# A later copy of the values' product, unread products before the MLP, and a last batch like the others: top-k attention and a channel MLP on one core

## The chip, the core and the metric

The kernel runs on one core of a Trainium2 chip. The metric is the time of one execution on the device, in microseconds (us). The kernel before takes 1666.45 us, the median of three executions (1665.65 to 1667.94). The execution that was profiled has a span of 1666.6 us. The engines are called PE (TensorE's matmuls; PEld are its weight loads), DVE (VectorE), ACT (ScalarE), POOL (GpSimd) and SP (SyncE, which starts most of the transfers).

## What is computed

Attention over 8 batches, 8 heads, 576 rows and a head dimension of 64, in which each row keeps only its 32 largest scores. The heads are then laid side by side (512 columns), and each row goes through a layer norm and an MLP of 512 to 2048 to 512 with a residual. All of it is in fp32.

```python
# attention: q, k, v are (8, 8, 576, 64)
scores = scale * np.matmul(q, k.transpose(0, 1, 3, 2))
kth = np.partition(scores, -32, axis=-1)[..., -32:-31]
scores = np.where(scores >= kth, scores, -1000000000.0)
scores = scores - np.max(scores, axis=-1, keepdims=True)
attn = np.exp(scores)
attn = attn / (np.sum(attn, axis=-1, keepdims=True) + 1e-09)
attn_out = np.matmul(attn, v)

# bridge, then the MLP: g_ln (512), w_ch1 (512, 2048), w_ch2 (2048, 512)
x = attn_out.transpose(0, 2, 1, 3).reshape(8, 576, 512)
mu = np.mean(x, axis=-1, keepdims=True)
var = np.mean((x - mu) ** 2, axis=-1, keepdims=True)
xn = (x - mu) / np.sqrt(var + 1e-06) * g_ln
out = x + np.maximum(xn @ w_ch1, 0.0) @ w_ch2
```

## The kernel before

The rows of a batch are cut into tiles of 128: numbers 0 to 3, and a rest of 64 rows, number J = 4. A **unit** is one tile for one pair of heads. There are 160 units, and the program is one loop over steps, one unit a step on DVE, with the other engines' work for the units before and after it written between. Nothing reorders the program: each engine takes its instructions in the order in which they stand in it.

A unit goes through these stages: `scores` (PE, with copies out of PSUM by ACT), `halve` and `select` (the 32 largest by rounds of MAX8 and MATCH_REPLACE8 on DVE, with two subtractions on POOL), `mask` and `weigh` (ACT: Prelu, then Exp with the row sum), and `turn` or `move` (the weights transposed, by PE and ACT or by DVE and DMA). Units of one batch and pair of heads form a **group**, and a group has one values' product:

```python
def values(g):
    vb = g.job.v
    av = brief("av")                       # a PSUM bank; five of these rotate
    for c in range(J):
        for h in range(2):
            nc.tensor.matmul(av[h * D : (h + 1) * D, 0 : g.nq], vb[:, h * J + c, :],
                             g.blocks[:, h, 0 : g.nq // 32, c, :], start=(c == 0), stop=False)
    nc.tensor.matmul(av[:, 0 : g.nq], g.job.ends[:], g.pt[:, 2 * J, 0 : g.nq],
                     start=False, stop=True)
    g.oT = otpool.tile([P, GQ], FP32, tag="oT", name="oT")
    nc.scalar.copy(g.oT[:, 0 : g.nq], av[:, 0 : g.nq])

def place(g):
    b, hp = g.job.b, g.job.hp
    for i, qt in enumerate(g.qts):
        if qt == J:
            ...                            # a copy of 64 columns on POOL
            continue
        ...
        ps = brief("xo")
        nc.tensor.transpose(ps[:, 0:P], g.oT[:, i * P : (i + 1) * P], ident[:])
        put(xs[b, qt], ps, hp * P, g.den, 2 * qt)     # two multiplications on ACT
```

When all pairs of heads of a tile are placed, the tile joins a **block** of one to three tiles for the MLP. A block's work is a list of items with a cost each, `todo`; `give` appends it at a fixed step, and `fill`, which is called eight times a step, takes items off the list as long as the allowance `owed` lasts. A `turn` item is four transposes on PE and a copy to xT on ACT. A `hidden` item is one 128-row product into hps; the last of each PSUM bank is followed by a relu on ACT. A `project` item is one product into ops; the last of each tile is followed by a scaling on ACT into o.

```python
def fill(least=0):
    owed[0] = min(owed[0] + share[0], 6.0)
    while todo and (not todo[0][3] or todo[0][3]()):
        if owed[0] < todo[0][1] / 2 and least <= 0:
            break
        least -= 1
        pop()                              # owed[0] -= cost; the item's instructions

# costs: turn 0.44, hidden max(1.71e-3 * N, 0.31) with N columns, project 1.71e-3 * 512

def slot(n):                               # share of one fill in step n
    if n <= CONVERTING:                    # CONVERTING = 17
        return max(0.0, dve_cost(n) - pe_cost(n)) / SLOTS       # SLOTS = 8
    left = sum(t[1] for t in todo)
    if n > last_give:
        even = left / max(1, END - 1 - n)
    else:
        even = 99.0
        for m in sorted(gives):
            if m > n:
                even = min(even, (left - RESERVE) / (m - n))    # RESERVE = 4.0
                left += sum(b.cost() for b in gives[m])
    return max(0.0, even) / SLOTS
```

The first block is given in step 9 (`gives_first`). Until then `todo` is empty. The order of the units comes from this list; `[0, 1]` and so on are the tiles of one group:

```python
for b in range(B):
    parts = [[0, 1], [2, 3], [J]]
    if b:
        parts = [[0, 1], [2, 3]]
        if b == B - 1:
            parts = [[J]] + parts
        else:
            parts[b < 2].append(J)
    for qts in parts:
        jobs += [Job(b, hp, [qts]) for hp in range(NHP)]     # NHP = 4 pairs of heads
...
for u in units[jobs[5 * NHP].first :]:                       # from batch 2 on
    u.moved = not u.rest and u is not u.group.units[-1]
```

A unit that is `moved` has its weights transposed by DVE and DMA. The others are transposed on PE, eight transposes for the two heads besides one for the last columns. The rests of an even and the following odd batch are put together to one tile, which joins the block of the odd batch's group that holds J; where that group holds nothing else, it is a block of one tile.

One step, cut to the order in which the calls concerned stand (ex is the unit of two steps ago, mk that of one step ago, g the group whose last unit came three steps ago):

```python
    for x in due(n): scores(x)
    ...
    fill()
    ...
    fill()
    if g: values(g)
    if parts and not moved: parts[0]()     # turn of ex, first head
    ...                                    # select, halve, the weights' conversion
    fill()
    if mk and not early: mask(mk, 0)
    if g: place(g)
    ...
    fill(1 if g or late else 0)
    fill()
    if len(parts) > 2: parts[1]()
    ...
```

Of the kernel before, what the change touches and what calls it, by code (L numbers as in the profile page):

```python
# [11 lines left out]
FP32 = mybir.dt.float32  # L12
# [9 lines left out]
J = 4  # L22
# [7 lines left out]
def kernel(  # L30
# [41 lines left out]
    nc = tc.nc  # L72
    P = nc.NUM_PARTITIONS
    B, H, S, D = q.shape
# [15 lines left out]
    GQ = 2 * P + R  # L90
# [11 lines left out]
    otpool = pool("ot", 1)  # L102
# [22 lines left out]
    def product(name):  # L125
        return mmps.tile([P, 512], FP32, tag="mm", name=name)
# [5 lines left out]
    ident = const([P, P], "ident")  # L132
# [72 lines left out]
    now = [-1]  # L205
# [38 lines left out]
    share = [0.0]  # L244
    owed = [0.0]

    def done(step):
        return step is not None and step < now[0]

    def pop():  # L250
        kind, cost, run, may = todo.pop(0)
        assert not may or may()
        owed[0] -= cost
        run()
# [5 lines that stand above are left out]
                break  # L260
            least -= 1
            pop()

# [273 lines left out]
    def values(g):  # L539
        vb = g.job.v  # L540
        av = brief("av")
        for c in range(J):
            for h in range(2):
                nc.tensor.matmul(  # L544
                    av[h * D : (h + 1) * D, 0 : g.nq],
                    vb[:, h * J + c, :],
                    g.blocks[:, h, 0 : g.nq // 32, c, :],
                    start=(c == 0),
                    stop=False,
                )  # L550
        nc.tensor.matmul(  # L551
            av[:, 0 : g.nq], g.job.ends[:], g.pt[:, 2 * J, 0 : g.nq],
            start=False, stop=True,
        )
        g.oT = otpool.tile([P, GQ], FP32, tag="oT", name="oT")
        nc.scalar.copy(g.oT[:, 0 : g.nq], av[:, 0 : g.nq])  # L556

    def put(dst, ps, c0, den, d0):
        for h in range(2):
# [6 lines left out]
    def place(g):  # L566

        b, hp = g.job.b, g.job.hp
        for i, qt in enumerate(g.qts):
            if qt == J:  # L570
                if b % 2 == 0:
                    oTr[hp] = restpool.tile([P, P], FP32, tag=f"oTr{hp}", name="oTr")
                r0 = R * (b % 2)
                nc.gpsimd.tensor_copy(
                    oTr[hp][:, r0 : r0 + R], g.oT[:, i * P : i * P + R]
                )
                continue
            if (b, qt) not in xs:
                pair = xpool.tile([P, 2, DM], FP32, tag="x", name="x")
                for j in range(2):  # L580
                    xs[b, qt // 2 * 2 + j] = pair[:, j]
            ps = brief("xo")
            nc.tensor.transpose(ps[:, 0:P], g.oT[:, i * P : (i + 1) * P], ident[:])
            put(xs[b, qt], ps, hp * P, g.den, 2 * qt)
# [145 lines left out]
    for b in range(B):  # L730
        parts = [[0, 1], [2, 3], [J]]
        if b:
            parts = [[0, 1], [2, 3]]
            if b == B - 1:
                parts = [[J]] + parts
            else:
                parts[b < 2].append(J)
        for qts in parts:
            jobs += [Job(b, hp, [qts]) for hp in range(NHP)]
    units = []  # L740
# [36 lines left out]
    for j in jobs:  # L777
        if j.hp == NHP - 1:
            b = j.b
# [67 lines left out]
    def give(n):  # L847
        early = not all(map(done, ready))
        for blk in gives[n]:
            rows, hidden, project = blk.items()  # L850

            at_end = 0 if early else 6
            kept, last = todo[: len(todo) - at_end], todo[len(todo) - at_end :]
            assert all(t[0] == "project" for t in last)
            todo[:] = kept + rows + last + hidden + project

    def slot(n):


        if n <= CONVERTING:  # L860
            return max(0.0, dve_cost(n) - pe_cost(n)) / SLOTS
# [7 lines that stand above are left out]
                    even = min(even, (left - RESERVE) / (m - n))  # L869
                    left += sum(b.cost() for b in gives[m])  # L870
        return max(0.0, even) / SLOTS
# [8 lines left out]
    gives_first = min(gives)  # L880
# [13 lines left out]
    for n in range(END):  # L894
        now[0] = n
        if n in gives:
            give(n)
        share[0] = slot(n)
        u, nxt, mk = at(n), at(n + 1), at(n - 1)
        ex, g = after(n)  # L900
        g = g if g and not g.quick else None
        late = at(n - 4)
        late = late if late and late.rest and late.job.b % 2 else None
        parts = turn(ex) if ex else []
        early = ex is not None and n - 1 < EARLY
        last = ex and ex is ex.group.units[-1]
        quick = ex.group if last and ex.group.quick else None

        moved = ex is not None and ex.moved
        sent, stores[:] = stores[:], []  # L910

        if ex and not early:
            weigh(ex, 0)
        for x in due(n):
            scores(x)
        if u:
            select(u, 0)
        for store in sent:
            store()
        if n == gives_first:  # L920
            for blk, i in rows_of.pop(n):
                blk.stats(i)
        if mk and mk.i >= CONVERTING:
            prepare(mk)
        if early:
            for t in range(2):
                mask(ex, t)
                weigh(ex, t)
        if not quick:
            weights(n, 0)  # L930
        fill()
        if ex and len(ex.tiles) > 1 and not early:
            weigh(ex, 1)
        fill()
        if g:
            values(g)
        if parts and not moved:
            parts[0]()
        if ex and ex.rest:
            keep_den(ex)  # L940
        if u:
            select(u, 1)
        if nxt:
            halve(nxt)
        for den in recips.pop(n, []):
            nc.vector.reciprocal(den, den)
        if n in turns:
            turn_heads(turns[n])
            later = fresh.index(turns[n]) + 1
            if later < len(fresh):  # L950
                load(fresh[later], nc.sync, nc.sync)
        if not quick:
            weights(n, 1)
        fill()
        if mk and not early:
            mask(mk, 0)
        if g:
            place(g)
        if late:
            place_rest(late.job.b, late.job.hp)  # L960
        fill(1 if g or late else 0)
        fill()
        if len(parts) > 2:
            parts[1]()
        if u:
            select(u, 2)
        for blk, i in rows_of.pop(n, []):
            blk.stats(i)
        for blk in gives.get(n - 2, []):
            blk.inverse()  # L970
        if last and ex.group.sums is not None:
            recips.setdefault(n + 1, []).append(ex.group.sums)
        last_rest = at(n - 3)
        if last_rest and last_rest.rest and last_rest.job.b % 2:
            hp = last_rest.job.hp
            den = dr[last_rest.job.b // 2][:, 2 * hp : 2 * hp + 2]
            recips.setdefault(n + 1, []).append(den)
        fill()
        if parts:
            parts[-1]()  # L980
        if mk and len(mk.tiles) > 1 and not early:
            mask(mk, 1)
        fill()
        for x in (u if n < EARLY else None, mk if n > EARLY else None):
            if x and x is units[x.job.last]:
                load_values(x.job)
        if quick:

            values(quick)
            for den in recips.pop(n + 1):  # L990
                nc.vector.reciprocal(den, den)
            place(quick)
            weights(n, 0)
            weights(n, 1)
        if u:
            select(u, 3)
            if u.i < CONVERTING:
                prepare(u)
        if moved:
            move(ex)  # L1000
        for x in (g, quick):
            if x and x.job.hp == NHP - 1:
                for qt in x.qts:
                    if qt < J:
                        arrived(n, (x.job.b, qt), xs[x.job.b, qt])
        if late and late.job.hp == NHP - 1:
            r = late.job.b // 2
            arrived(n, ("r", r), rs[r])
        fill()
# [37 lines left out]
```

## Time and profile before

| engine | busy us | share of the span | instructions |
|---|---|---|---|
| PE | 1566.9 | 94% | 7057 |
| PEld | 941.7 | 57% | 7057 |
| DVE | 1469.6 | 88% | 4611 |
| ACT | 1042.4 | 63% | 2615 |
| POOL | 671.5 | 40% | 881 |

| work on PE (half-products: a product of fp32 is two instructions) | count | busy us |
|---|---|---|
| hps, 256 columns | 1664 | 399.5 |
| hps, 384 columns | 384 | 137.4 |
| hps, 128 columns | 128 | 16.4 |
| ops, 512 columns | 1152 | 548.0 |

How to read it: the shares are averages over the whole span, and the stages differ. Busy times of overlapping instructions are counted once for an engine but not across rows, so that the rows of a table may add up to more than the engine's line. Matmuls overlap in the trace: the duration of one is longer than the time until the next can start, which is why the spacing of starts is of more use than the mean duration. The mean granted clock of PE is 0.978 of the full one. A wait in the profile is idle time of an engine, put down to what released it; it costs something only where that engine, or one that waits for it, sets the pace.

### The profile page before, as it was taken

The page shows a single profiled execution, that of the slowest core. Times are in us where ns is not written, and L with a number is a line of the kernel's source. Part 1 is how long each engine was busy: PE and PEld are TensorE (multiplying, and loading weights), DVE is VectorE, ACT ScalarE, POOL GpSimd, SP SyncE. Part 2 cuts the span into 40 slices and gives each one's busy share as a digit, 9 for nine tenths or more (in the row PEclk, how much of TensorE's full clock was granted, in tenths as well). Part 3 has the DMA queues.
Part 4 walks back from the last instruction along what each step waited for, and adds up shares of the span by engine and source line. Part 5 has one row for each costly group of instructions (what it writes and reads, how often), then busy time and mean ns, then how long its engine had stood idle before and what let it go on. Part 6 is the DMA issues. An engine that isn't in the chain of part 4 may idle for free.

```text
span 1666.6 us, 24932 instructions
## 1 busy us (share of the span) xinstructions
PE 1566.9 (94%) x7057; PEld 941.7 (57%) x7057; DVE 1469.6 (88%) x4611; ACT 1042.4 (63%) x2615; POOL 671.5 (40%) x881
## 2 busy tenths in 40 slices
PE   2668989989899999999999999999999999999998
PEld 1336457556355474745547575745547575756764
DVE  5997999999999999999999999999879895988600
ACT  6886877667556665666656665656555565666620
POOL 5776763343442433343243433443243423333110
PEclk9879999999999999999999999999999999999999
DMA  7423332001442335333443335324333251222200
GB/s 176 106 72 95 85 64 58 21 14 22 100 110 84 99 85 132 93 88 89 108 123 92 86 104 126 97 71 99 99 97 97 72 115 46 61 78 70 80 13 13
DMA packets 303185, 139.30 MB, mean 84 GB/s; under 512 B 250820, under 2 KB 285640, under 8 KB 303048
## 3 DMA queue, kind: packets, MB, share of 16 engines
q1 hardware_dynamic: 298312, 137.12, 31.2%
q10 hardware_dynamic: 4736, 0.59, 0.3%
q8 instruction: 57, 0.93, 0.2%
q14 instruction: 80, 0.66, 0.1%
HBM read 92.54 MB, written 45.09 MB: 83 GB/s over the span
## 4 chain that ended last, share of the span: by engine, by line
PE 65%; DVE 23%; ACT 4%; issue 4%; POOL 3%; DMA 1%; SPq 0%; ACTq 0%; POOLq 0%; DVEq 0%
PE hps L664 23%; PE ops L680 22%; PE scps L354 7%; DVE m L399 7%; PE av L544 6%; DVE hi L386 6%; DVE hi L391 3%; DVE lo L386 2%; PE tp L490 2%; PE av L551 2%; DVE hi L375 2%; DVE size L193 1%; ACT sc L335 1%; POOL lo L376 1%; ACT e L426 1%
## 5 line engine op out<-in xcount | busy, mean ns | idle before, releaser
L664 PE MATMUL hps<-xT,w 128*128 128x256 f32 (+2 forms) x2176 | 553.3, 398 | 6.0 <-ACT xT L653 6.0
L680 PE MATMUL ops<-w,h 128*128 128x512 f32 x1152 | 548.0, 603 | 0.0
L399 DVE MAX8 m<-hi 128x8 f32<-128x304 f32 x1152 | 487.6, 458 | 3.3
L664 PEld LDWEIGHTS hps<-xT,w 128*128 128x128 f32 x2176 | 388.8, 192 | 111.4 <-issue 32.3
L376 POOL TENSOR_TENSOR lo<-sc,hi 128x576 int32<-128x576 int32 (+1 forms) x160 | 207.8, 1299 | 486.3 <-DVE hi L375 246.5
L386 DVE MATCH_REPLACE8 hi<-m,hi 128x304 f32<-128x304 f32 x864 | 389.4, 456 | 0.0
L680 PEld LDWEIGHTS ops<-w,h 128*128 128x128 f32 x1152 | 201.2, 192 | 187.2 <-issue 182.7
L391 DVE MAX8 hi<-lo 128x8 f32<-128x288 f32 x576 | 233.7, 441 | 39.3 <-POOL lo L379 38.2
L354 PE MATMUL scps<-kT,qT 64*128 64x288 f32 (+3 forms) x1344 | 220.7, 429 | 37.1 <-DVE qT L306 27.4
L335 ACT COPY sc<-scps 128x288 f32<-128x288 f32 x576 | 199.7, 408 | 68.2 <-PE scps L354 55.9
L426 ACT ACTIVATE e<-sc,m 128x576 f32<-128x576 f32 x288 | 224.1, 779 | 7.2 <-DVE m L399 4.0
L436 ACT ACTIVATE e<-e,bias 128x576 f32<-128x576 f32 x288 | 224.8, 781 | 0.7
L379 POOL TENSOR_TENSOR lo<-lo,sc 128x576 int32<-128x576 int32 (+1 forms) x160 | 206.9, 1293 | 12.5
L354 PEld LDWEIGHTS scps<-kT,qT 64*128 64x128 f32 (+1 forms) x1344 | 122.3, 179 | 152.9 <-issue 57.6
L544 PE MATMUL av<-pt,vb 128*64 128x256 f32 (+2 forms) x1152 | 148.8, 401 | 0.2 <-ACT pt L513 0.2
L675 ACT ACTIVATE h<-hps 128x512 f32<-128x512 f32 (+1 forms) x156 | 88.5, 567 | 86.1 <-PE hps L664 84.8
L375 DVE TENSOR_TENSOR hi<-sc 128x576 f32<-128x576 f32 (+1 forms) x160 | 115.0, 719 | 23.4 <-ACT sc L335 23.4
L556 ACT COPY oT<-av 128x256 f32<-128x256 f32 (+2 forms) x72 | 26.8, 372 | 160.3 <-PE av L551 160.3
L693 POOL TENSOR_TENSOR o<-o,x 128x512 f32<-128x512 f32 x32 | 42.0, 1313 | 209.6 <-ACT o L689 209.6
L386 DVE MATCH_REPLACE8 lo<-hi,lo 128x288 f32<-128x288 f32 x288 | 125.2, 441 | 0.0
L490 PE MATMUL tp<-ident,e 128*128 128x128 f32 x608 | 97.0, 284 | 25.3 <-ACT e L436 24.8
L544 PEld LDWEIGHTS av<-pt,vb 128*64 128x64 f32 x1152 | 76.0, 142 | 78.5 <-ACT sc L335 14.5
(70 smaller groups left out, 1259.5 us busy)
## 6 DMA issues: line engine op xcount, KB each, us to landing
turned<-sc SPq DMA_DIRECT2D x68, 512.0 KB, 2.6
pt<-turned SPq DMA_DIRECT2D x272, 128.0 KB, 3.0
vb<-in_v_dram SPq DMA_DIRECT2D x144, 128.0 KB, 2.6
raw<-in_moe_w_ch_dram SPq DMA_DIRECT2D x32, 512.0 KB, 4.0
kin<-in_k_dram SPq DMA_DIRECT2D x128, 72.0 KB, 2.5
qin<-in_q_dram SPq DMA_DIRECT2D x120, 72.0 KB, 2.5
out_dram<-o SPq DMA_DIRECT2D x32, 256.0 KB, 2.2
ends<-in_v_dram SPq DMA_DIRECT2D x144, 16.0 KB, 2.2
```

The costliest lines, as they stand in the source:

```text
L335: nc.scalar.copy(u.sc[:, t, s * HALF : (s + 1) * HALF], made[s][t][:, 0:HALF])
L354: nc.tensor.matmul(ps[i * R : i * R + ql, o : o + width], qT[r, q0 : q0 + ql], kT[r, k0 : k0 + width], start=True, stop=True,)
L376: nc.gpsimd.tensor_tensor(lo.bitcast(I32), a.bitcast(I32), hi.bitcast(I32), ALU.subtract)
L379: nc.gpsimd.tensor_tensor(lo.bitcast(I32), lo.bitcast(I32), b.bitcast(I32), ALU.add)
L386: nc.vector.match_replace(x[:, t], m[:, t, :], x[:, t], LOWEST)
L391: nc.vector.max(u.hi[:, t, o : o + 8], u.lo[:, t])
L399: nc.vector.max(m[:, t, :], u.hi[:, t])
L426: nc.scalar.activation(u.e[:, t], u.sc[:, t], AF.Prelu, bias=u.thr[:, t, 7:8], scale=-1.0, alpha=SLOPE)
L436: nc.scalar.activation(u.e[:, t], u.e[:, t], AF.Exp, bias=u.bias[:, t : t + 1], scale=-scale / SLOPE, accum_out=g.den[:, col : col + 1],)
L544: nc.tensor.matmul(av[h * D : (h + 1) * D, 0 : g.nq], vb[:, h * J + c, :], g.blocks[:, h, 0 : g.nq // 32, c, :], start=(c == 0), stop=False,)
L664: nc.tensor.matmul(ps["h"][:, o : o + N], w1[:, c, f * P : (f + 1) * P], xT[0][:, c, 0:N], start=(c == 0), stop=(c == NC - 1),)
L680: nc.tensor.matmul(ps[i][:], hT[f][:, i * P : (i + 1) * P], w2[:, f, :], start=(f == 0), stop=(f == NF - 1),)
```

## The change

Three things are changed.

The copy of the values' product out of PSUM moves from the end of `values` to the beginning of `place`. Between the two stand a turn of another unit (where it isn't moved), a fill, and a mask. It is meant to keep ACT from standing in front of a product that PE hasn't finished.

As long as the MLP has not begun, the allowance that nothing uses is spent on products of the identity with itself, which nobody reads; one for each 0.62 of it. They are meant to keep PE from idling, and so its clock up. In the step in which the first block is given, the allowance is set to its ceiling, 6.0.

In the last batch the rest no longer comes first and alone, but in a group with tiles 0 and 1, as in batches 2 to 6.

```diff
@@ -244,6 +244,14 @@
+    WARM = 0.62
+
+    def warm():
+
+        ps = product("warm")
+        nc.tensor.matmul(ps[:, 0:P], ident[:], ident[:], start=True, stop=True)
+
     def done(step):
         return step is not None and step < now[0]
@@ -260,6 +268,10 @@
                 break
             least -= 1
             pop()
+        if now[0] < gives_first:
+            while owed[0] > WARM:
+                owed[0] -= WARM
+                warm()
@@ -552,8 +564,7 @@
             av[:, 0 : g.nq], g.job.ends[:], g.pt[:, 2 * J, 0 : g.nq],
             start=False, stop=True,
         )
-        g.oT = otpool.tile([P, GQ], FP32, tag="oT", name="oT")
-        nc.scalar.copy(g.oT[:, 0 : g.nq], av[:, 0 : g.nq])
+        g.av = av
@@ -566,6 +577,8 @@
     def place(g):
 
         b, hp = g.job.b, g.job.hp
+        g.oT = otpool.tile([P, GQ], FP32, tag="oT", name="oT")
+        nc.scalar.copy(g.oT[:, 0 : g.nq], g.av[:, 0 : g.nq])
         for i, qt in enumerate(g.qts):
@@ -731,10 +744,7 @@
             parts = [[0, 1], [2, 3]]
-            if b == B - 1:
-                parts = [[J]] + parts
-            else:
-                parts[b < 2].append(J)
+            parts[b < 2].append(J)
         for qts in parts:
@@ -895,6 +905,8 @@
         if n in gives:
             give(n)
+        if n == gives_first:
+            owed[0] = 6.0
         share[0] = slot(n)
```

## The prediction

> **What bounds the kernel now.** I began with the page's forty slices, to see which engine is full where and at what clock.
>
> ```profile
> PE   2668989989899999999999999999999999999998
> DVE  5997999999999999999999999999879895988600
> PEclk9879999999999999999999999999999999999999
> ```
>
> Three stages. In the first three slices (about 125 us) DVE is full, PE is not, and PE's clock is low. In the middle both are full. From slice 29 on DVE has slack and in the last two PE is alone. The busy time of each engine by stretch of 10 us (then of 40 us) puts numbers on it; after the length of the stretch come PE, PEld, DVE, ACT and POOL busy with counts, then the granted clock.
>
> ```profile
> 70.00:80.00 10.00, 7.52 (x27) 4.11 (x29) 10.00 (x33) 9.56 (x20) 6.58 (x6) 0.50 0.54 98
> 90.00:100.00 10.00, 7.00 (x21) 3.51 (x23) 10.00 (x36) 9.53 (x22) 7.74 (x7) 0.52 0.39 117
> 130.00:140.00 10.00, 10.00 (x45) 8.70 (x44) 5.84 (x23) 4.25 (x8) 4.48 (x5) 0.93 0.18 52
> ```
>
> ```profile
> 1000.00:1040.00 40.00, 40.00 (x157) 20.06 (x154) 39.66 (x126) 23.49 (x63) 16.29 (x26) 1.00 0.52 129
> 1200.00:1240.00 40.00, 40.00 (x144) 18.78 (x143) 33.61 (x108) 20.57 (x53) 13.45 (x19) 1.00 0.41 116
> ```
>
> From 480 us on PE has 39.4 to 40.0 of nearly every 40 us. Busy time alone does not prove a full PE, so I looked at start-to-start spacing in the timeline. In the tail, where only PE works, 128 half-products of 256 columns start between 1605.94 and 1633.67, 0.217 us each. In the middle, around 1048 us, four of them start between 1048.90 and 1049.76, 0.215 each. They run at the tail's rate, so PE is the limit, and **from 480 us on every microsecond added to or taken from PE's queue is a microsecond of the kernel**. Before 120 us it is DVE's microseconds that count; between 130 and 480 the two share.
>
> **What the Trainium skill says.** *TensorE: Matmul & The Clock Gate*, Part 1 (The HAM clock gate), says that PE starts at half clock, is released by a window of activity of 3.4 us and falls back after an idle one, and that only half and full exist. The trace agrees: stretches at 0.50 above, and eight score products of unit 1 (starting at 12.88 us) take 2.29 us against 1.24 at 1000 us. The same page's Part 2 says that matmuls stay in program order. *Perfetto Trace Analysis*, Per-instruction lifecycle, says that ACT is "strict FIFO". The trace bears on this: ACT idles 160 us in front of the copy that is moved, with other work behind it. The last two statements decide what moving a copy does.
>
> **Part 1, the copy of the values' product.** The waits view shows what the change aims at (total us, times, longest).
>
> ```profile
> ACT oT L556 <- PE av L551: 160.3, 64, 5.7
> ```
>
> ACT is only 63% busy and does not bound, so these 160 us are worth nothing by themselves. What counts is whether PE's next instruction that needs the copy, the transpose xo, comes later. The usual case, ACT's timeline:
>
> ```profile
> 791.04 0.37 ACT L556 COPY oT<-av 128x256 f32<-128x256 f32 x1 [2.55 <-PE av L551]
> 791.31 0.78 ACT L426 ACTIVATE e<-sc,m 128x576 f32<-128x576 f32 x1
> 791.99 0.92 ACT L560 ACTIVATE x<-xo,den 128x64 f32<-128x64 f32 x4
> ```
>
> The change puts the mask (L426, 0.78) ahead of the copy. ACT idles 2.55 us before the copy, and the mask's inputs are old (comparing the last MAX8 of each unit with its mask, I find a median of 9 us), so the mask slips into the idle time and the copy still starts when av ends. No gain, no loss. The other case is where the fill between values' product and place ends with something that ACT must answer:
>
> ```profile
> 729.84 0.43 ACT L556 COPY oT<-av 128x320 f32<-128x320 f32 x1 [3.20 <-PE av L551]
> 730.70 0.78 ACT L689 ACTIVATE o<-ops,mv,rstd 128x512 f32<-128x512 f32 x1 [0.43 <-PE ops L680]
> 731.38 0.76 ACT L426 ACTIVATE e<-sc,m 128x576 f32<-128x576 f32 x1
> ```
>
> On PE the transpose stands at 730.50. After the change ACT's order is o at 730.70, mask at 731.38, then the copy at about 732.05, done at 732.48: PE would stand 2.0 us at xo. With a relu or xT in that place the same sum gives 1.6 to 1.8. To count these places I followed the kernel's pacing arithmetic (share, owed, the costs in the items) through its steps. It gives an order, no times, and for the kernel before it names seven places, which are the seven where ACT's timeline has such an instruction behind the copy (466, 729, 749, 771, 1048, 1188 and 1558 us). For the changed order it names five: one near 466 us (DVE's stage, half absorbed), o, xT and relu at 729 to 771, and one o in the last batch. So 2.0 + 1.6 + 1.7 + 2.0 = **7.3 us** of new PE waiting. In batches 0 and 1 the units' turning also stands between (a pt copy of 0.59 and the mask), and xo waits about 1 us in some dozen places. There PE is not the limit, its own waits for x (4.3 us at 344, 5.3 us at 457) can take the delay up, and I allow **+2.5**.
>
> **Part 2, the products of the constant.** The same walk gives 99 of them in steps 0 to 8, each two instructions of 128 columns, 0.11 us apiece at full clock (the chain has 20 such in 2.23 us): 22 us in the first 120, where PE is idle about 57. They replace idle time, and much of PE's own work there should halve. But DVE is at 10.00 of 10 from 30 to 120 us, so this moves nothing until the MLP begins. There the trace shows a cost of the low clock:
>
> ```profile
> 127.31 13.49 PE L664 MATMUL hps<-xT,w 128*128 128x256 f32 x52 [2.97 <-ACT xT L653]
> ```
>
> ```profile
> 143.03 0.76 DVE L375 TENSOR_TENSOR hi<-sc 128x576 f32<-128x576 f32 x1 [7.19 <-ACT sc L335]
> ```
>
> 52 at the tail's 0.217 would take 11.3 us, so 2.2 us are lost here, and some tenths in the turning of x before; DVE then stands 7.19 us for scores queued behind these products. Being in DVE's stage, that is a real gain: **-3**. Setting owed to 6.0 only restores what it had already reached.
>
> **Part 3, the last batch.** Four units of 64 rows no longer stand alone.
> - Values: each lone group costs PE 0.89 us (start 1433.72 to 1434.61) and about 0.09 for changing kind; the same columns within a group of 320 cost 2.37 - 1.95 + 0.11 = 0.53. Four times 0.45 = -1.8.
> - Hidden layer: a block of one tile (128 x 0.11 = 14.1) and one of two (128 x 0.217 = 27.7) become one of three (128 x 0.325, by columns, = 41.6): -0.2. It is a wash, though the kernel's own cost table would promise 6.
> - Second tiles of [0, 1] are no longer the last of their group, so they are moved by DVE and DMA instead of turned on PE: four units x eight transposes x 0.108 = -3.5 on PE, +5.5 on DVE, which has slack there.
>
> Sum **-5.5 on PE**. The pacing also changes: with the last one-tile block gone, the walk hands out 6.4 cost units a step up to step 155 instead of 7.4 from step 116, then 12.2. That is a shift between stretches in which PE is full either way (39.5 to 40.0 of 40 at both rates), so I give it 0.
>
> **The sum.** +7.3 + 2.5 - 3 - 5.5 = +1.3 on 1666.45. I put the figure at 1667.
>
> **Rivals.**
> 1. *The freed wait pays.* If ACT's 160 us were on the path, relus and score copies would come earlier and some 10 to 20 us could be won: about 1650. For it: the wait is ACT's longest. Against: after 480 us PE's waits for ACT come to only some 7 us, so there is nothing to win them from.
> 2. *PE's waits grow instead.* Every one of the 63 places could wait 1 us or more if the mask came late: +60 us, 1725. Against it: the mask's inputs are some 9 us old and ACT has over 1.2 us free before the copy almost everywhere. A mild form, more relu places than I count, would give 1675.
> 3. *The constant's products get in the way.* If PE stays at half clock they cost twice, 45 us of the 57 idle, and scores for the next unit come late to a DVE that has no slack: +5 to +10.
> 4. *The slower pacing starves PE.* At 6.4 a step PE and DVE are balanced (in 1000 to 1040 DVE has 39.66), so a batch and a half more of it could leave PE idle 1% of 430 us, +4, and the fuller last steps end later.
>
> **Range and chances.** The terms are each good to 3 to 5 us, which together make some 10: 1656 to 1679. A change of 2% is 33 us, which only a strong form of rival 2 (slower) or of 1 (faster) reaches: 0.03 each.
>
> **What would show it.** ACT's wait for av at the copy shrinks little (the mask takes some 0.7 us of each); PE's wait at xo grows from 7.0 us by 8 to 20, in a handful of long ones after 480 us and a dozen of 1 us before; the clock is 1.00 in most stretches from 20 to 120 us; DVE's wait at 143 is 4 to 5 us; PE has about 7023 matmuls (+198 -72 -128 -32); DVE falls below 30 of 40 only after about 1560. Wrong if DVE waits for scores before 120 us, if PE idles in 1160 to 1560, or if xo waits at more than ten places after 480.

## The result, and the profile after

The changed kernel takes 1675.35 us, the median of four executions (1673.7 to 1677.43), against 1666.05 for the kernel before in the same series. The ratio is 1.0056, with a 95% interval of 1.0039 to 1.0073: **9 us slower, within 2%**. The prediction of 1667 (1656 to 1679) holds as a range. Its figure is 8 us off, and that is no accident of small terms: three of its four terms were mis-sized beyond the noise (the copy before 480 us, the unread products and the last batch).

In what follows, "us against before" is (ratio - 1) times 1667, since every run is compared by its ratio to the kernel before, run beside it on the same chip; the ranges in brackets are 95% intervals. The page's slices of the changed kernel:

```profile
PE   4669789989989999999999999999999999999998
DVE  5997889999999999999999999999999999997000
PEclk7899899999999999999999999999999999999999
```

PE does more before 120 us (74.1 us busy where it had 62.8, by the unread products), DVE has lost some of slices 5 and 6, and DVE's slack of slices 29 to 37 is gone: it now runs ahead and is done three slices before the end. Three of the stretches shown of before and one late one, in the changed kernel (the columns are the stretch, its length, the busy us of PE, PE's loads, DVE, ACT and GpSimd with their instructions, the granted clock, the DMA share and GB/s):

```profile
70.00:80.00 10.00, 7.25 (x40) 4.96 (x40) 10.00 (x32) 9.53 (x20) 7.38 (x7) 0.77 0.58 110
90.00:100.00 10.00, 6.24 (x39) 4.67 (x39) 10.00 (x37) 9.87 (x22) 8.13 (x7) 0.97 0.36 104
130.00:140.00 10.00, 10.00 (x47) 8.48 (x47) 4.58 (x18) 5.34 (x9) 4.71 (x5) 1.00 0.17 52
1200.00:1240.00 40.00, 40.00 (x146) 18.96 (x147) 39.65 (x126) 22.98 (x60) 15.23 (x25) 1.00 0.49 128
```

The clock is higher before 120 us, and DVE is as full there as it was: nothing to win, as the prediction said. In the last stretch DVE has 39.65 of 40 where it had 33.61, by the slower pacing. The waits at the copy, first the one for xo in the kernel before, then two of the changed kernel (total us, times, longest):

```profile
PE xo L583 <- ACT oT L556: 7.0, 8, 2.0
```

```profile
ACT oT L581 <- PE av L563: 82.6, 45, 3.2
PE xo L596 <- ACT oT L581: 36.5, 24, 6.6
```

ACT's wait in front of the copy is halved, and PE's wait for the copy has grown from 7.0 us in 8 places to 36.5 in 24. Of ACT's saved 78 us, 67 came back in other waits: those for the turns' products, for hidden products and for xo rose from 35.4 to 56.1, from 84.8 to 103.1 and from 2.3 to 30.6. Where PE waits longer than 1 us at xo, in the list of PE's waits in order of time: 63, 85 and 106 us (before the MLP, where it costs nothing), **175 (5.07) and 204 (6.59)**, then 240, 291 and 374 (1.2 to 1.7), and after 480 us just four, at 742 (1.85), 763 (1.61), 785 (1.51) and 1493 (1.85). The four are those that the prediction had counted, at 2.0, 1.6, 1.7 and 2.0. ACT and then PE at the first of them, from the timeline of the changed kernel (start in us, length, engine, line, instruction, and in brackets the idle time before it and what ended it):

```profile
740.91 0.78 ACT L702 ACTIVATE o<-ops,mv,rstd 128x512 f32<-128x512 f32 x1 [4.05 <-PE ops L693]
741.59 0.76 ACT L438 ACTIVATE e<-sc,m 128x576 f32<-128x576 f32 x1
742.26 0.41 ACT L581 COPY oT<-av 128x320 f32<-128x320 f32 x1
```

```profile
742.72 0.44 PE L596 MATMUL xo<-ident,oT 128*128 128x128 f32 x2 [1.85 <-ACT oT L581]
```

The copy stands behind o and the mask, although its product had been ready since 740.0. The two long ones are another matter. ACT (two lines), PE and DVE in the step of the first, in the kernel before:

```profile
170.86 0.37 ACT L556 COPY oT<-av 128x256 f32<-128x256 f32 x1 [0.28 <-PE av L551]
175.12 0.68 ACT L187 ACTIVATE sign<-raw 128x512 f32<-128x512 f32 x1 [2.08 <-POOL w L201]
```

```profile
171.53 0.38 PE L583 MATMUL xo<-ident,oT 128*128 128x128 f32 x2
```

```profile
181.05 0.76 DVE L375 TENSOR_TENSOR hi<-sc 128x576 f32<-128x576 f32 x1 [1.60 <-ACT sc L335]
```

The same step in the changed kernel:

```profile
171.28 0.66 ACT L184 ACTIVATE low<-raw 128x512 f32<-128x512 uint32 x1
174.04 0.67 ACT L187 ACTIVATE sign<-raw 128x512 f32<-128x512 f32 x1 [2.11 <-POOL w L201]
174.61 0.77 ACT L438 ACTIVATE e<-sc,m 128x576 f32<-128x576 f32 x1
175.28 0.35 ACT L581 COPY oT<-av 128x256 f32<-128x256 f32 x1
```

```profile
175.69 0.69 PE L596 MATMUL xo<-ident,oT 128*128 128x128 f32 x2 [5.07 <-ACT oT L581]
```

```profile
184.22 0.76 DVE L387 TENSOR_TENSOR hi<-sc 128x576 f32<-128x576 f32 x1 [5.83 <-ACT sc L347]
```

Here the conversion of a weight (L183, L184, L187) stands between the product, ready at 169.75, and the copy, and its third activation waits 2.11 us for GpSimd. That wait is in the kernel before too, but there the copy came ahead of it. PE stands at xo meanwhile, the next unit's scores are queued behind xo, and DVE stands 5.83 us for them instead of 1.60.

Profiles of kernels that don't differ before 120 us differ by some 2 us there (DVE ends unit 8 between 116.1 and 118.4 us in e5, e6, e9 and e10; the runs e1 to e11 are described in the next section). So I compare this stage by the time that DVE takes from the end of unit 8 to its first MAX8 of unit 22 (end to end, of those that read `hi`), called **stage E** below: 144.7 us before, 154.2 after the change. Stage E is a single trace's, and has a spread of its own: e3 and e8, which are the same program as the kernel before up to there, take 142.7 and 143.1. It can't tell less than 2 us. The two units concerned can be told better. DVE takes 12.9 us for unit 13 and 10.3 for unit 15 (from the last MAX8 of the unit ahead to its own) in all of before, e2 to e5 and e8; in the changed kernel it takes 17.1 and 15.1, which is 9.0 of the 9.5.

### The profile page after: what moved, and what is told of

Same layout as the page of the kernel before. It is cut to its first block, busy times and chain, and to the rows that moved or that the text cites. A ratio compares the mean times of both kernels' runs of the same rounds, so it can differ in the third digit from the quotient of the medians.

```text
span 1673.3 us, 24863 instructions
## 1 busy us (share of the span) xinstructions
PE 1570.0 (94%) x7023; PEld 936.7 (56%) x7023; DVE 1474.2 (88%) x4619; ACT 1046.3 (63%) x2607; POOL 675.9 (40%) x879
## 4 chain that ended last, share of the span: by engine, by line
PE 77%; DVE 10%; ACT 6%; issue 4%; POOL 2%; DMA 1%; ACTq 0%; POOLq 0%; DVEq 0%
PE hps L677 27%; PE ops L693 25%; PE scps L366 9%; PE av L556 7%; PE tp L502 3%; DVE m L411 3%; PE av L563 2%; DVE hi L398 2%; DVE hi L403 1%; ACT e L438 1%; PE xo L596 1%; ACT sc L347 1%; DVE lo L398 1%; DVE hi L387 1%; DVE size L193 1%
## 5 line engine op out<-in xcount | busy, mean ns | idle before, releaser
L677 PE MATMUL hps<-xT,w 128*128 128x256 f32 (+1 forms) x2048 | 551.5, 413 | 3.4 <-ACT xT L666 3.4
L411 DVE MAX8 m<-hi 128x8 f32<-128x304 f32 x1152 | 498.7, 478 | 3.3
L677 PEld LDWEIGHTS hps<-xT,w 128*128 128x128 f32 x2048 | 373.2, 192 | 120.3 <-issue 31.1
L398 DVE MATCH_REPLACE8 hi<-m,hi 128x304 f32<-128x304 f32 x864 | 398.0, 476 | 0.0
L403 DVE MAX8 hi<-lo 128x8 f32<-128x288 f32 x576 | 238.4, 456 | 15.0 <-POOL lo L391 13.9
L366 PE MATMUL scps<-kT,qT 64*128 64x288 f32 (+3 forms) x1344 | 207.6, 420 | 26.6 <-DVE qT L318 16.3
L366 PEld LDWEIGHTS scps<-kT,qT 64*128 64x128 f32 (+1 forms) x1344 | 116.4, 175 | 136.3 <-issue 61.0
L688 ACT ACTIVATE h<-hps 128x512 f32<-128x512 f32 (+1 forms) x160 | 89.2, 557 | 104.3 <-PE hps L677 103.1
L556 PE MATMUL av<-pt,vb 128*64 128x256 f32 (+2 forms) x1088 | 142.5, 405 | 0.0
L480 DVE STREAM_TRANSPOSE sc<-e 128x512 f32<-128x512 f32 x144 | 95.2, 698 | 24.1 <-ACT e L448 23.8
L556 PEld LDWEIGHTS av<-pt,vb 128*64 128x64 f32 x1088 | 71.5, 139 | 73.9 <-ACT sc L347 12.9
L502 PEld LDWEIGHTS tp<-ident,e 128*128 128x128 f32 x576 | 72.6, 144 | 59.1 <-issue 22.9
```

The source lines that it names most:

```text
L366: nc.tensor.matmul(ps[i * R : i * R + ql, o : o + width], qT[r, q0 : q0 + ql], kT[r, k0 : k0 + width], start=True, stop=True,)
L398: nc.vector.match_replace(x[:, t], m[:, t, :], x[:, t], LOWEST)
L403: nc.vector.max(u.hi[:, t, o : o + 8], u.lo[:, t])
L411: nc.vector.max(m[:, t, :], u.hi[:, t])
L677: nc.tensor.matmul(ps["h"][:, o : o + N], w1[:, c, f * P : (f + 1) * P], xT[0][:, c, 0:N], start=(c == 0), stop=(c == NC - 1),)
```

## The experiments

**e1, the copy alone.** The kernel before, with `g.av = av` in `values` and the copy at the head of `place`, as in the change.

> The kernel before with only the copy moved. Theory A (the copy is late wherever ACT has something else between): the old order has six places after 480 us in which ACT answers a fill before it copies, together about 10 us; the two steps in which half of a weight's conversion also stands between (12 and 14) cost DVE 4 to 5 us each; the turning in batch 1 about 1 us. Sum 1686, with two PE waits of 5 us or more at xo near 171 and 200 us. Theory B (the prediction's own sizes, 2.5 us for everything before 480): 1678 to 1679. Theory C (the copy is innocent, the early loss comes from the unread products): 1666.

Measured: 1690.51 us, ratio 1.0137 (1.0123 to 1.0151), 23 us against before. Stage E takes 154.9 us, as in the changed kernel. After 480 us xo waits at seven new places, in the old order: 1.85, 1.61, 1.50, 1.66, 1.50, 0.81 and 1.61. The copy alone costs more than the whole change, and the loss is not from the unread products. That it costs 23 here and 18 in the changed kernel (against e5) is mostly a matter of which places the pacing makes: the last batch's new order leaves four, with 6.8 us of waits where the seven here have 10.5.

**e2, the unread products alone**, with the line that sets the allowance to 6.0.

> The kernel before with only the unread products. Theory A: the first hidden product starts 0.8 us earlier and DVE's later waits for scores come 1.1 us earlier, so 1665. The prediction: 1663. Theory C (they stand in the way of DVE's scores): 1670 or more.

```diff
+        if now[0] < gives_first:
+            while owed[0] > WARM:
+                owed[0] -= WARM
+                warm()
```

Measured: 1667.55 us, ratio 0.9998 (0.9990 to 1.0006). They do nothing that can be measured, neither good nor harm. Stage E is 143.1 us.

**e3, the last batch alone.**

> The kernel before with only the last batch changed. The prediction's sum: 5.5 us of PE's work saved, 1660.5. By the distance between the two traces, which shrinks by about 7 in the last batch beside a new wait: 1659. Rival (the slower pacing starves PE between 1160 and 1560 us): 1666 or more, with PE below 39 of 40 there.

```diff
-            if b == B - 1:
-                parts = [[J]] + parts
-            else:
-                parts[b < 2].append(J)
+            parts[b < 2].append(J)
```

Measured: 1658.57 us, ratio 0.9949 (0.9937 to 0.9962), 8.5 us won. The stretch from 1160 to 1560 us, first in the kernel before and then in this one (columns as above):

```profile
1160.00:1560.00 400.00, 397.12 (x1895) 246.42 (x1894) 348.36 (x1101) 236.22 (x602) 139.89 (x202) 1.00 0.31 82
```

```profile
1160.00:1560.00 400.00, 398.68 (x1704) 232.27 (x1704) 357.47 (x1119) 240.98 (x618) 139.22 (x199) 1.00 0.33 93
```

PE is as full at the slower pacing as at the faster one, so the rival falls: a shift between full stretches costs nothing that can be seen. Adding up PE's spacing by kind from 470 us on, the values' products cost 1.3 us less, the turns 4.3, and its waits 2.3.

**e8, the last batch, but with tile 1 turned on PE.**

> The last batch alone changed, but tile 1 of it turned on PE and not moved, as before. By the prediction's count 32 transposes of 0.108 come back: 3.5 us more than with the last batch alone, 1662 to 1663. If what was won there is the pacing or the values' products: no difference, 1659.

```diff
+        if u.job.b == B - 1 and u.qt == 1:
+            u.moved = False
```

Measured: 1663.21 us, ratio 0.9973 (0.9962 to 0.9985), 4 us (1 to 7) of the 8.5 given back. PE's spacing says the same: the turns cost 3.5 us more than in e3. So some half of what the last batch wins is that four more units are transposed by DVE and DMA instead of PE. The group of instructions that counts them (total us and mean ns behind the bar), first in e3 and then in e8:

```profile
L490 PE MATMUL tp<-ident,e 128*128 128x128 f32 x576 | 91.8, 284 | 25.9 <-ACT e L436 25.4 <-ACT sc L335 0.5
```

```profile
L490 PE MATMUL tp<-ident,e 128*128 128x128 f32 x608 | 96.7, 284 | 25.9 <-ACT e L436 25.4 <-ACT sc L335 0.5
```

**e4, the copy late from step 18 on only.** The changed kernel, with the copy back in `values` while weights are converted.

> The changed kernel, with the copy where it was in the steps up to 17, in which weights are converted. Theory A: the two waits of 5.1 and 6.6 us at xo go, 9 us are won, 1666. Theory B (the early place costs 2.5 at most): 1673. Theory C: no difference, 1675.

```diff
+        if now[0] <= CONVERTING:
+            take(g)                  # in values: the copy, where it was
...
+        if now[0] > CONVERTING:
+            take(g)                  # in place
```

Measured: 1664.17 us, ratio 0.9980 (0.9972 to 0.9988), 12.7 us less than the changed kernel. Stage E is 142.9 us, 11.4 less. The early steps are what the prediction got most wrong.

**e5, products and last batch, the copy where it was.**

> The changed kernel with the copy back in its old place everywhere: products and last batch alone. If the parts add up: 1666 - 1 - 7 = 1658, and 8 us less than the run with the copy late after step 17 only. By the prediction's sizes: 1657.5. If the copy's freed wait were worth anything, this would be slower than that.

Measured: 1659.05 us, ratio 0.9949 (0.9937 to 0.9961). Against e4 this is 5.2 us less, for waits that sum to 1.85 + 1.61 + 1.50 + 1.85 = 6.8 us in e4's trace. Where they may differ can be seen at the first hidden product of the block at 757 us, in the timeline of e5 and then of e4:

```profile
755.44 2.85 PE L675 MATMUL hps<-xT,w 128*128 128x384 f32 x8 [1.95 <-ACT xT L664]
```

```profile
757.02 3.17 PE L683 MATMUL hps<-xT,w 128*128 128x384 f32 x9 [0.22 <-ACT xT L672]
```

PE would have stood there for xT anyway; having stood 1.61 us at xo just before, it stands only 0.22. So a new wait took the place of an old one, and 6.8 - 1.7 = 5.1. That this meets 5.2 so well is luck, since the 5.2 is good to 2.4 us.

**e7, the mask behind place.** The changed kernel with two calls exchanged.

> The changed kernel with the mask behind place instead of ahead of it; the copy still stands behind the fill and, early on, behind the conversion. Theory A: each of the five waits at xo behind an answered fill is 0.67 us shorter, about 3 us after 480, those of batch 1 with only a turning between (0.75 to 1.2 us) nearly vanish, the two of steps 12 and 14 stay above 4 us: 1671. If the mask alone makes the copy late: 1666. If it has no part: 1675.

```diff
+        if g:
+            place(g)
         if mk and not early:
             mask(mk, 0)
-        if g:
-            place(g)
```

Measured: 1670.42 us, ratio 1.0017 (1.0011 to 1.0024), 6.5 us less than the changed kernel. The four late waits are 1.19, 0.95, 0.84 and 1.19, shorter by 0.66 each, as expected. Stage E is 150.9 us, 3.3 less, more than I had thought: the waits of 5.07 and 6.59 fell to 4.35 and 5.94, and DVE's behind them from 5.83 and 5.37 to 4.04 and 4.47.

**e11, the copy behind the conversion, ahead of fill and mask.** The changed kernel with `take(g)` after `weights(n, 1)` in the step.

> The changed kernel with the copy behind the turn and the conversion of the weights, but ahead of the fill and the mask. Theory (in steps 12 and 14 the conversion, which waits for GpSimd, is what makes the copy late; after 480 us it is the answered fill and the mask): the waits of about 4.4 and 5.9 us near 175 and 203 us stay, those after 480 us go, 1667 to 1668. If the mask or the fill made the early ones too: all waits go, 1659. If it is neither: 1675.

Measured: 1664.70 us, ratio 0.9988 (0.9980 to 0.9996), some 3 us better than expected. ACT's timeline in the same step as above:

```profile
175.68 0.67 ACT L187 ACTIVATE sign<-raw 128x512 f32<-128x512 f32 x1 [2.12 <-POOL w L201]
176.25 0.36 ACT L553 COPY oT<-av 128x256 f32<-128x256 f32 x1
```

PE waits 4.41 and 5.94 us at xo there, and nowhere longer than 1.01 after 205 us. Stage E gives the ladder of what stands between product and copy in these steps: 142.9 to 143.8 us with nothing (e4, e5), 149.5 behind turn and conversion (e11), 150.9 with the fill (e7), 154.2 with the mask too (the change). Units 13 and 15 give it without the spread: 12.9 and 10.3 us, then 15.2 and 14.2, 15.3 and 14.2, and 17.1 and 15.1. So of their 9.0 us about 6.2 come with turn and conversion, nothing that can be seen with the fill, and 2.7 with the mask. Of turn and conversion it is mostly the conversion: in the changed kernel's timeline the turn's copy to pt ends at 170.81, and the conversion only at 174.71. Putting the conversion itself behind place was not tried.

**e6, unread products until the first hidden product.** e5 with 5 of them behind the first turning of x in step 9 and 8 behind the second.

> As the run before, with 13 more unread products in step 9: 5 behind the first turning of x and 8 behind the second, where PE idles 0.8 and 1.9 us. Theory D (the clock falls at 124 us because the products end one step too early): it stays full, the first 52 half-products of the MLP take 11.3 us in place of 13.2, DVE's wait for scores near 142 us shrinks by 2, and 2 us are won: 1656. Rival (the clock falls on what PE did before 120 us, or the products delay xT): no gain, 1658 to 1659.

PE and DVE at the beginning of the MLP, from the timeline of the changed kernel (two extracts), then from that of e6 (two):

```profile
126.51 13.22 PE L677 MATMUL hps<-xT,w 128*128 128x256 f32 x52 [1.90 <-ACT xT L666]
```

```profile
141.97 0.76 DVE L387 TENSOR_TENSOR hi<-sc 128x576 f32<-128x576 f32 x1 [7.38 <-ACT sc L347]
```

```profile
126.94 11.46 PE L679 MATMUL hps<-xT,w 128*128 128x256 f32 x52 [0.43 <-issue]
```

```profile
140.64 0.76 DVE L387 TENSOR_TENSOR hi<-sc 128x576 f32<-128x576 f32 x1 [5.62 <-ACT sc L347]
```

The granted clock stands in the columns as above, third from the end, for e5 and then for e6:

```profile
120.00:130.00 10.00, 6.44 (x21) 5.08 (x22) 9.93 (x33) 4.67 (x11) 8.46 (x8) 0.66 0.56 159
```

```profile
120.00:130.00 10.00, 7.41 (x52) 6.56 (x49) 9.86 (x28) 6.84 (x15) 8.27 (x8) 1.00 0.48 159
```

So it was the clock: with PE kept busy through step 9 the 52 half-products take 11.46 us and not 13.22 as in the changed kernel or 13.77 as in e5, and DVE waits 1.8 or 2.3 us less. The products of the change end with step 8; PE then idles 2.18, 0.79 and 1.90 us within 8, and the clock falls. In the kernel's time the gain is not resolved: 1658.70 us, ratio 0.9945 (0.9933 to 0.9957) against e5's 0.9949.

**e9 and e10, no reset of the allowance.** e5 and e6 without the line `owed[0] = 6.0`.

> Products and last batch (the run of 1659.05 us), without the line that sets the allowance to 6.0 in step 9, so that the first block's work starts at the pace of the steps. If DVE's 7 to 8 us of waiting near 141 us come from the 26 hidden products that the allowance lets in ahead of the next scores: that wait falls below 2 us and, since DVE sets the pace until 430 us, 4 to 6 us are won, 1654. Rival (the burst is needed, the work left out is missing later, or the wait returns in the following steps): 1658 to 1660.

> The same with the 13 further products of step 9. If the clock matters beside the burst, 1 to 2 us less than the run without them; if only the burst matters, no difference.

Measured: e9 1655.63 us, ratio 0.9931 (0.9919 to 0.9944); e10 1657.05, ratio 0.9938 (0.9924 to 0.9951). In e9 30 half-products instead of 52 stand ahead of the next scores, and DVE waits 3.74 us instead of 7.92, more than the 2 expected, since the clock is low again and the 30 take 9.61 us. In e10, with the clock kept up, they take 6.71 and DVE waits 1.64. Stage E is 139.4 and 136.5 us against 143.8 and 142.7 with the reset. Both are the fastest of the series, 10 to 12 us under the kernel before, but each is apart from its partner by only 1 to 3 us, with intervals that overlap. The two can't be told apart from each other. That the reset costs something in its stage is shown by the stage; how much of it reaches the end is not settled.

## Why the prediction was right as a range, and where its steps failed

| term | predicted, us | measured, us | by |
|---|---|---|---|
| copy, after 480 us | +7.3 | +5.2 (2.8 to 7.6) | e4 less e5: from step 18, about 226 us, on |
| copy, before 480 us | +2.5 | +12.7 (9.5 to 15.8) | the change less e4: up to step 17 |
| unread products | -3 | -0.3 (-1.7 to +1.0) | e2 |
| last batch | -5.5 | -8.5 (-10.5 to -6.3) | e3 |
| sum | +1.3 | +9.1 | the change: +9.3 (6.5 to 12.2) |

The intervals of the first two rows are the half-widths of the two runs' intervals, added as squares. The runs part the copy's cost at step 18 and not at 480 us; what xo waits between these two falls into the first row.

That the sum stayed inside 1656 to 1679 is in part luck. The early copy was 10 us off, where each term was held to be good to 3 to 5. The late copy and the last batch came out 2 and 3 us better than predicted; without them it would have been about 1680.

**What bounds.** Right: PE after 480 us, DVE before 120. The change's higher clock before 120 us moves nothing there, and saved PE time in the last batch is saved time.

**The copy after 480 us.** Right in place and mechanism, four out of four, and each wait within 0.2 us. The interval of 2.8 to 7.6 leaves room for the sum of 7.3. If it was too high, the trace of e4 says why: a wait was added to the path without asking what PE would wait for next (xT at 757).

**The copy before 480 us.** This is the step that failed: "I allow +2.5". It named the pt copy and the mask as what comes between, and forgot the conversion of the weights. The list of what stands between, in the section on the change, lacks it too; the step shown further up has it, in one line between values and place, and in steps 12 and 14 a second piece of it falls there. The argument against rival 2, that ACT has over 1.2 us free ahead of the copy almost everywhere, holds for 49 of the 54 copies after 480 us but only for 12 of the 24 earlier ones, and at 171 us it was 0.28. The prediction also reasoned that PE is not the limit there and its own waits take the delay up. In batch 1 that is what the traces show: xo waits 0.75 to 1.2 us in seven places, and DVE takes as long from its first MAX8 of unit 22 to the 301st of the kernel (those that read `hi`; 165.3 us) as before (165.8). It fails in steps 12 and 14: of PE's waits of 5.07 and 6.59 us, 4.2 and 4.8 came through to DVE. The program makes scores one unit ahead there and two from step 18 on, which would explain it; but the waits of batch 1 are shorter too, and no run changed how far ahead scores are made, so this part is not shown.

**The unread products.** "-3" rested on the clock being full when the MLP begins. The products end one step too soon for that (e6). PE's idle times between 118 and 128 us, in the trace of the kernel before 1.29, 1.39 and 2.97 us, come after step 8, the last that has such products.

**The last batch.** The count of moved tiles was right (4 us against 3.5), and so was the finding that merging the block of one tile is a wash. Missing were 2.3 us of PE's own waits in the old order of the last batches.

**What was to be seen.** Matmuls: 7023, as counted. ACT's wait at the copy: halved, not little changed. PE's wait at xo: grown by 29.5, not 8 to 20. DVE's wait near 142 us: 7.38, not 4 to 5. Clock: 1.00 in two of the ten stretches from 20 to 120 us, not in most, and 0.50 to 0.97 in the others. DVE below 30 of 40: from 1520 on, not 1560. None of the three signs of being wrong showed (DVE's waits for scores before 120 us are those of the kernel before), although a step had failed: they looked at DVE before 120 us and at PE late in the kernel, and the loss lay between. Rival 1 (the freed wait pays) and rival 3 (the products get in the way) are refuted by e1 and e2, rival 4 by e3. Rival 2 in its mild form has the right figure, 1675, but not the cause: the loss came from the early steps and not from more relus.

## What to carry to other kernels

Moving an instruction later on an engine with slack is not free: what counts is everything that stands ahead of it in its new place, and above all whether any of that waits for a third engine. Before allowing for absorption, look how far ahead the next consumer of the stalled engine is supplied; here, with one unit ahead, 9.0 us of 11.7 came through. And a wait that an engine will have anyway a few microseconds later can take up a new one, so new waits should be summed along the engine's timeline and not as a list.

## What the runs showed of the hardware

Clock and activity: the share of time that PE is busy did not tell the granted clock of a stretch. From 60 to 70 us the clock was 1.00 in the changed kernel, with PE busy 5.08 of 10 us, but 0.83 in e7 with 6.46 and 0.66 in e11 with 6.49.

Clock and stalls: from 200 to 210 us, where the longer of the two early stalls at xo lies (5.94 to 6.60 us), the clock was 0.66 or 0.67 in the changed kernel, e1, e7 and e11, and 1.00 in the kernel before and in e3 to e6, which don't have the stall. From 170 to 180, around the shorter one, the two sets are not apart: 0.72 to 0.83 with it, 0.79 to 1.00 without.

Change of kind on PE: in the kernel before, from 480 us on, the next instruction starts 0.429 us (median) behind a half-product of ops when it is another of ops, a hidden product, a turn or xo, but 0.522 us behind it when it is a score or a values' product (74 places). The first of ops behind scores holds PE for 0.533 (50 places). Scores and values' products are those that the trace lists with 64*128 and 128*64 where it has 128*128 for the others; the prediction's 0.09 for changing kind is theirs.
